# Moving the start of the big buffer to a multiple of 256 bytes, and of the accumulator to a multiple of 64, in a decode kernel that streams its key and value cache

## The chip, the cores and the metric

The kernel runs on one core of a Trainium2 chip. The metric is the device time of one execution in microseconds (us), lower being better. Times are medians of several executions; the profile is one further execution, recorded by the hardware profiler.

## What is computed

One token is decoded. Its normalised vector goes through attention over a long cache and, beside that, through a small mixer and MLP; the results are summed.

```python
def _A_ref(x, k_cache, v_cache, wq, wo):          # Hq 32, Hkv 4, Sk 65536, Dh 128, D 1024
    q = (x @ wq).reshape(B, Sq, Hq, Dh).transpose(0, 2, 1, 3)
    k = jnp.repeat(k_cache, rep, axis=1)           # 8 query heads share one key/value head
    v = jnp.repeat(v_cache, rep, axis=1)
    scores = jnp.einsum("bhqd,bhkd->bhqk", q, k) * (Dh ** -0.5)
    o = jnp.einsum("bhqk,bhkd->bhqd", _softmax(scores), v)
    return o.transpose(0, 2, 1, 3).reshape(B, Sq, Hq * Dh) @ wo

def _B_ref(x, w1, w2, w3, w4):                     # F 3584
    h = _gelu(_layernorm(x) @ w1)
    hs = shifted_quarters_of(h) @ w2               # one position only, so the shifts give zeros
    x1 = x + hs
    return x1 + _gelu(_layernorm(x1) @ w3) @ w4

x = A_x
xn = _layernorm(x)
return x + _A_ref(xn, A_k_cache, A_v_cache, A_wq, A_wo) + _B_ref(xn, B_w1, B_w2, B_w3, B_w4)
```

Nearly all of the bytes are the cache: 4 heads x 65,536 positions x 128 values x 2 bytes, once for K and once for V, are 134 MB of the 170 MB that are read. The rest is weights.

## The kernel before, in words

The kernel is written engine by engine. Small queue objects (`_Q`) collect each engine's instructions with the semaphore waits that follow from buffer objects (`_B`), and the order of work is written out by hand. There is no scheduler that could reorder it.

**Memory.** SBUF tensors are allocated one after the other with `sb(...)` (lines 217 to 261), each starting on a multiple of 32 bytes of the partition. The last is `KV` (line 261), 196,608 bytes of each of the 128 partitions. Everything large is loaded into it. It holds two K buffers and two V buffers of 32,768 bytes (`KOFF`, `VOFF`, line 262), a region for transposed K (`XOFF`), and a region for weights (`WOFF`). All of these offsets, and the places of the weights, are multiples of 256 bytes from KV's start.

**Loads.** SP issues all large transfers, `issue_k` and `issue_v` through line 335 and the weights through line 323. A K or V transfer is 4,096 KB: 16,384 positions of a head, 128 of them in each partition, one contiguous 32,768-byte run per partition. First come wq, K 0, V 0 and K 1; then, as buffers come free, K and V in turn; near the end w1, w2, w3, wo and w4, the last in four parts (line 646) into KV.

**The loop.** One sub-block is 8,192 positions, half of a transfer, and there are 32 of them (`for n in range(NT)`, line 584):

- `Ttr` (line 490): four VectorE transposes of K inside KV, 128x1024 words each, one sub-block ahead.
- `QK` (line 500): 16 TensorE matmuls from the transposed K in KV into `S_ps`.
- `stats1`, `MB`, `stats2` (lines 509 to 519) and `EXP` (lines 528 to 534): the running bound of the softmax on VectorE, the exponential on ScalarE into `p_sb`, with the row sums going to `tmpO`.
- `PTr` (lines 538 and 540): a TensorE permutation and a VectorE transpose of the probabilities into `pT_f`.
- `PV` (line 548): 16 matmuls of V in KV into `OT_ps`.
- `FLASH` (lines 556 to 561): ScalarE copies `OT_ps` to `tmpO`; POOL scales the accumulator `O_acc` by `ff` (line 559) and adds `tmpO` (line 561). At the end of a head, POOL folds `O_acc` into `keep` (`head_end`, lines 566 to 576).

SP's issue of the next K or V transfer stands at the end of a sub-block and waits for the reader of the buffer that it overwrites: the transposes of line 490 for K, the matmuls of line 548 for V.

**The end.** Attention's result goes through `keep` and `o_bf` into the rows of wo (line 660), followed by the rows of w4 (lines 660 and 452) as its parts land; sums go to `OUT_ps` (line 691), and line 696 copies the result for the last DMA.

**Start bytes in a partition, from the built program:** `KV` 31,552, which is 123 x 256 + 64. `O_acc` 26,400, which is 412 x 64 + 32. `tmpO` 20,096, `p_sb` 22,176, `pT_f` 24,224, `keep` 28,480.

Of the kernel before, what the change touches and what calls it, by code (L numbers as in the profile page):

```python
# [6 lines left out]
BF = mybir.dt.bfloat16  # L7
F32 = mybir.dt.float32
# [156 lines left out]
def _dma(q, chan, fn, reads=(), writes=(), partial=False):  # L165
    _deps(q, reads, writes)
    chan.n += 1
    ev = q.dma(fn, chan.sem, 16 * chan.n)
    _done(ev, reads, writes, partial)
    return ev  # L170


def bass_parallel_sum__gqa_block_cached__mixer_s_mlp__decode_kernel(
# [13 lines left out]
    P = 128  # L187
# [17 lines left out]
    with ExitStack() as es:  # L205
        E = es.enter_context

        def sb(name, shape, dt):
            return E(nc.sbuf_tensor(name, shape, dt))
# [30 lines left out]
        qT_bf = sb("qT_bf", [P, HQ], BF)  # L240
        Yall = sb("Yall", [P, HKV, 4, 4, G], BF)
        Ycur = sb("Ycur", [P, 4, 4, G], BF)
        tmpO = sb("tmpO", [P, 520], F32)
        p_sb = sb("p_sb", [P, 2, 512], BF)
        pT_f = sb("pT_f", [P, 512], F32)
        mrow = sb("mrow", [P, 2], F32)
# [11 lines left out]
        acc = sb("acc", [P, KT_D], F32)  # L258
        g_bf = sb("g_bf", [P, KT_D], BF)
        gh_bf = sb("gh_bf", [P, KT_F], BF)  # L260
        KV = sb("KV", [P, 98304], BF)
        KOFF, VOFF, XOFF, WOFF = (0, 32768), (16384, 49152), 65536, 81920
        EPI = KV[:, 45056:49152].bitcast(F32)
        Dmat_f, Pmat_f = EPI[:, 1024:1152], EPI[:, 1152:1280]
# [29 lines left out]
        def chan(name):  # L294
            if name not in chans:
                chans[name] = _DmaChan(sem("d_" + name))
            return chans[name]
# [27 lines left out]
        _dma(q_act, chan("x"), lambda e: e.dma_start(out=x_bf[:, :], in_=A_x[0, 0, :].rearrange("(p j) -> p j", p=P)), writes=[b_x])  # L325
        wq_sb = KV[:, VOFF[1]:VOFF[1] + 8 * HQD]
        b_wq = [b_V[1]] + b_X[0] + b_X[1]
        load_rows(wq_sb, b_wq, "wq", A_wq, 0, 8)

        def issue_kv(m, cache, off, bufs, ch):  # L330
# [3 lines left out]
            src = cache[0, h, nb * 2 * SUB:(nb + 1) * 2 * SUB, :].rearrange("(p c) d -> p (c d)", p=P)  # L334
            _dma(q_sp, chan("%s%d" % (ch, m % 2)), lambda e: e.dma_start(out=KV[:, off:off + 16384], in_=src), writes=bufs)

# [142 lines left out]

        KV32 = KV[:].bitcast(F32)  # L480
        kstep = KV[:].ap[0][0]
        pT_bf = pT_f[:].bitcast(BF).rearrange("p (q r two) -> p q r two", q=16, two=2)
# [10 lines left out]
        def QK(n):  # L493
            xs = n % 2
            fns = []
            for we in range(4):
                w_hi, e_ = divmod(we, 2)
                for cm in range(4):
                    mv = bass.AP(KV[:].tensor, XOFF + xs * 8192 + cm * 128 + w_hi * 64 + e_, [[kstep, P], [512, 16], [2, 32]])
                    fns.append(lambda e, we=we, cm=cm, mv=mv: e.matmul(  # L500
# [232 lines left out]
```

## Time and profile before

| | |
|---|---|
| median of 3 runs | 402.64 us (402.51 to 402.99) |
| the profiled execution | 403.04 us, of which the span from first to last instruction is 401.7 us |
| read from device memory | 169.87 MB, 423 GB/s over the span |
| VectorE (DVE) busy | 238.7 us (59%), 403 instructions |
| TensorE (PE) busy | 183.4 us (46%), 1428 matmuls |
| GpSimd (POOL) busy | 92.2 us (23%), 175 instructions |
| ScalarE (ACT) busy | 49.7 us (12%), 132 instructions |
| mean granted TensorE clock | 0.635 of full speed |

The page of a profile lists, for one execution, busy times by engine, the span in 40 equal slices, the DMA queues, the chain of work that ended last, the costliest groups of instructions (line, engine, operation, output<-input, count, busy us, mean ns, idle time before and what ended it), and the large transfers with the time from issue to landing. The trace behind it can be asked for one line, one stretch of time or one queue, and it holds a record of every DMA packet with its bytes and duration. A busy share is a mean over stages with different limits, so the chain and the waits are read with it.

### The profile page before, as it was taken

To read this page: it belongs to the slowest core of one execution; us is meant where nothing else is said; L and a number is where in the kernel's file an instruction comes from. 1 tells how busy PE (TensorE), PEld (TensorE's weight loads), DVE (VectorE), ACT (ScalarE), POOL (GpSimd) and SP (SyncE) were. 2 spreads that over 40 slices of the span, in tenths; PEclk is the share of its full clock that TensorE was granted. 3 is DMA by queue.
4 is the path that set the end of the run, shared out by engine and by line. 5 is a ranking of instruction groups with operands and counts; after the bars stand their busy time and mean duration, and the time that the engine had idled before them with its cause. 6 is when DMAs were issued, how large, how long until landed. Compare 5 with 4: busy or idle time off the path is not lost.

```text
span 401.7 us, 4260 instructions
## 1 busy us (share of the span) xinstructions
PE 183.4 (46%) x1428; PEld 52.9 (13%) x1428; DVE 238.7 (59%) x403; ACT 49.7 (12%) x132; POOL 92.2 (23%) x175
## 2 busy tenths in 40 slices
PE   0043256463534444444444454545352636636557
PEld 0022011110111111111111011111010101212112
DVE  0024788667575758585768585858585858664201
ACT  1000011111111111111112020111111112100000
POOL 6000032231315222222432121216222222430000
PEclk9998556555655555656566555566566565585988
DMA  9989999999999999999999999999999999999995
GB/s 385 450 365 434 447 417 424 450 427 424 427 447 421 428 434 440 421 427 444 431 427 431 440 424 431 434 437 422 427 447 431 424 424 427 465 398 427 439 413 212
DMA packets 6209, 169.98 MB, mean 423 GB/s; under 512 B 820, under 2 KB 824, under 8 KB 952
## 3 DMA queue, kind: packets, MB, share of 16 engines
q1 hardware_dynamic: 6056, 169.87, 98.5%
q8 instruction: 4, 0.07, 0.1%
q14 instruction: 5, 0.04, 0.0%
q10 hardware_dynamic: 144, 0.00, 0.0%
HBM read 169.87 MB, written 0.00 MB: 423 GB/s over the span
## 4 chain that ended last, share of the span: by engine, by line
DMA 56%; DVE 19%; PE 11%; issue 11%; ACT 1%; POOL 0%; DVEq 0%; SPq 0%; ACTq 0%; POOLq 0%
DMA KV<-in_A_k_cache_dram 41%; DVE KV L490 12%; DMA KV<-in_B_w_dram 10%; DMA x_bf<-in_A_x_dram 6%; PE S_ps L500 5%; DVE mrow L509 3%; PE PT_ps L538 2%; PE S_ps L660 2%; ACT p_sb L530 1%; PE MB_ps L515 1%; DVE Bst L519 1%; DVE Rm L510 1%; DVE brun L528 1%; DVE pT_f L540 1%; PE OT_ps L548 0%
## 5 line engine op out<-in xcount | busy, mean ns | idle before, releaser
L490 DVE STREAM_TRANSPOSE KV<-KV 128x1024 f32<-128x1024 f32 x132 | 156.5, 1216 | 53.9 <-DMA KV<-in_A_k_cache_dram 53.9
L548 PE MATMUL OT_ps<-KV,pT_f 128*32 128x512 bf16 x512 | 60.7, 627 | 26.6 <-DVE pT_f L540 26.6
L500 PE MATMUL S_ps<-KV,Ycur 128*32 128x512 bf16 x512 | 59.2, 610 | 16.9 <-DVE KV L490 16.9
L561 POOL TENSOR_TENSOR O_acc<-O_acc,tmpO 128x516 f32<-128x516 f32 x32 | 41.3, 1290 | 95.8 <-ACT tmpO L556 95.8
L530 ACT ACTIVATE p_sb<-S_ps,brun 128x512 bf16<-128x512 f32 x32 | 22.0, 688 | 163.9 <-DVE brun L528 163.9
L515 PE MATMUL MB_ps<-Rm,Lmat 128*128 128x16 bf16 x32 | 6.2, 192 | 75.6 <-DVE Rm L510 75.6
L538 PE MATMUL PT_ps<-p_sb,permR 128*128 128x512 bf16 x32 | 18.3, 571 | 45.8 <-ACT p_sb L530 45.8
L556 ACT ACTIVATE tmpO<-OT_ps 128x512 f32<-128x512 f32 x32 | 19.1, 598 | 106.1 <-PE OT_ps L548 106.1
L558 POOL TENSOR_TENSOR spare<-ff 128x1 f32<-128x1 f32 x32 | 6.2, 193 | 113.1 <-ACT ff L534 113.0
L509 DVE TENSOR_REDUCE mrow<-S_ps 128x1 f32<-128x512 f32 x32 | 21.6, 675 | 16.5 <-PE S_ps L500 16.5
L540 DVE STREAM_TRANSPOSE pT_f<-PT_ps 128x512 f32<-128x512 f32 x32 | 22.7, 709 | 3.0
L500 PEld LDWEIGHTS S_ps<-KV,Ycur 128*32 128x32 bf16 x512 | 14.7, 125 | 62.1 <-issue 32.4
L548 PEld LDWEIGHTS OT_ps<-KV,pT_f 128*32 128x32 bf16 x512 | 14.8, 129 | 58.6 <-DVE pT_f L540 30.7
L559 POOL TENSOR_SCALAR O_acc<-O_acc,ff 128x520 f32<-128x520 f32 x32 | 22.3, 698 | 0.0
L515 PEld LDWEIGHTS MB_ps<-Rm,Lmat 128*128 128x128 bf16 x32 | 3.3, 102 | 103.0 <-DVE Rm L510 103.0
L381 PE MATMUL MM_ps<-ln_s,ones_f 128*128 128x1 f32 x6 | 1.8, 362 | 27.2 <-DVE ln_s L380 27.2
L689 DVE COPY KV<-S_ps 64x512 f32<-64x512 f32 x1 | 0.7, 683 | 22.1 <-PE S_ps L660 22.1
L377 DVE CAST xT<-x_bf 128x8 f32<-128x8 bf16 x1 | 0.2, 173 | 21.5 <-DMA x_bf<-in_A_x_dram 21.5
L660 PE MATMUL S_ps<-KV,o_bf 128*1 128x512 bf16 x64 | 8.9, 443 | 5.0 <-DMA KV<-in_A_wo_dram 5.0
L519 DVE TENSOR_REDUCE Bst<-MB_ps 128x1 f32<-128x16 f32 x32 | 5.6, 175 | 9.2 <-PE MB_ps L515 9.2
L393 POOL TENSOR_TENSOR ln_s<-ln_s,neghalf 128x1 f32<-128x1 f32 x3 | 1.7, 558 | 39.5 <-DVE ln_s L391 39.5
L538 PEld LDWEIGHTS PT_ps<-p_sb,permR 128*128 128x128 bf16 x32 | 3.3, 103 | 48.7 <-ACT p_sb L530 48.7
(116 smaller groups left out, 127.0 us busy)
## 6 DMA issues: line engine op xcount, KB each, us to landing
KV<-in_A_k_cache_dram SPq DMA_DIRECT2D x16, 4096.0 KB, 23.3
KV<-in_A_v_cache_dram SPq DMA_DIRECT2D x16, 4096.0 KB, 22.1
KV<-in_A_wo_dram SPq DMA_DIRECT2D x2, 4096.0 KB, 27.4
KV<-in_B_w_dram SPq DMA_DIRECT2D x1, 7168.0 KB, 20.9
KV<-in_B_w_dram SPq DMA_DIRECT2D x2, 2048.0 KB, 24.9
KV<-in_B_w_dram SPq DMA_DIRECT2D x1, 4096.0 KB, 41.3
KV<-in_B_w_dram SPq DMA_DIRECT2D x1, 1536.0 KB, 41.3
KV<-in_B_w_dram SPq DMA_DIRECT2D x1, 1024.0 KB, 43.4
```

The lines of the kernel that those rows point to most:

```text
L490: _op(q_dve, lambda e, c=c, x=x: e.transpose(out=KV32[:, x:x + 1024], in_=KV32[:, c:c + 1024]), reads=[b_K[s][half]], writes=[b_X[xs][ix]])
L500: fns.append(lambda e, we=we, cm=cm, mv=mv: e.matmul(S_ps[32 * cm:32 * cm + 32, :], Ycur[:, we, :, :].rearrange("p a g -> p (a g)"), mv, s ...
L509: _op(q_dve, lambda e: e.reduce_max(mrow[:, m:m + 1], S_ps[:, :], axis=AX.X), reads=[b_S], writes=[b_mrow[m]])
L515: _op(q_pe, lambda e: e.matmul(MB_ps[:, 0:16], Lmat[:, :], Rm[:, m, :], start=True, stop=True), reads=[b_R[m], b_const], writes=[b_MB])
L530: _op(q_act, lambda e: e.activation(p_sb[:, m, :], S_ps[:, :], ACTF.Exp, bias=brun[:, m:m + 1], scale=SCALE, accum_out=tmpO[:, cL:cL + 1]) ...
L538: _op(q_pe, lambda e: e.matmul(PT_ps[:, :], permR[:, :], p_sb[:, m, :], start=True, stop=True), reads=[b_p[m], b_const], writes=[b_PT])
L540: _op(q_dve, lambda e: e.transpose(out=pT_f[:, :], in_=PT_ps[:, :]), reads=[b_PT], writes=[b_pT])
L548: fns.append(lambda e, q=q, q4=q4: e.matmul(OT_ps[32 * q4:32 * q4 + 32, :], pT_bf[:, q, :, 1], KV[:, v0 + 512 * q:v0 + 512 * (q + 1)], sta ...
L556: _op(q_act, lambda e: e.activation(tmpO[:, 4:516], OT_ps[:, :], ACTF.Copy), reads=[b_OT], writes=[b_tmpO])
L559: b_Oacc.set_write(q_pool.op(lambda e: e.tensor_scalar(out=O_acc[:, :], in0=O_acc[:, :], scalar1=ff[:, m:m + 1], scalar2=0.0, op0=ALU.mult ...
L561: ev = q_pool.op(lambda e: e.tensor_tensor(out=O_acc[:, 4 * m:4 * m + 516], in0=O_acc[:, 4 * m:4 * m + 516], in1=tmpO[:, 4 * m:4 * m + 516 ...
L660: _grp(q_pe, [lambda e, lhs=lhs, rhs=rhs, jj=jj: e.matmul(S_ps[32 * jj:32 * jj + 1, :], lhs, rhs[:, 512 * jj:512 * jj + 512], start=False, ...
```

## The change

`tmpO` is allocated with 528 elements in place of 520, 32 bytes more, and a tensor `align` of 160 bytes, which nothing uses, is allocated ahead of `KV`. Everything allocated after `tmpO` moves up by 32 bytes, and `KV` by 192.

```diff
-        tmpO = sb("tmpO", [P, 520], F32)
+        tmpO = sb("tmpO", [P, 528], F32)
...
         gh_bf = sb("gh_bf", [P, KT_F], BF)
+        sb("align", [P, 80], BF)
         KV = sb("KV", [P, 98304], BF)
```

| tensor | start before | start after |
|---|---|---|
| `tmpO` | 20,096 (multiple of 64) | the same |
| `p_sb` | 22,176 (multiple of 64, plus 32) | 22,208 (multiple of 64) |
| `pT_f` | 24,224 (multiple of 64, plus 32) | 24,256 (multiple of 64) |
| `Rm` | 26,304 (multiple of 64) | 26,336 (multiple of 64, plus 32) |
| `O_acc` | 26,400 (multiple of 64, plus 32) | 26,432 (multiple of 64) |
| `keep` | 28,480 (multiple of 64) | 28,512 (multiple of 64, plus 32) |
| `brun` | 31,104 (multiple of 64) | 31,136 (multiple of 64, plus 32) |
| `o_bf` | 31,360 (multiple of 64) | 31,392 (multiple of 64, plus 32) |
| `KV` | 31,552 (multiple of 256, plus 64) | 31,744 (multiple of 256) |

No instruction is added, removed or reordered on any engine, and no other code changes.

## Prediction, made before the changed kernel had run

> **What bounds the kernel now.** I read the page from the top: engine shares first, then the slices and the queues. The busiest engine, VectorE (DVE), is busy 59% of the span; the transfers are another matter. These are the DMA lines of the page (busy tenths and GB/s in 40 slices of 10.04 us, then the main queue with its packets, MB and share of 16 DMA engines):
>
> ```profile
> DMA  9989999999999999999999999999999999999995
> GB/s 385 450 365 434 447 417 424 450 427 424 427 447 421 428 434 440 421 427 444 431 427 431 440 424 431 434 437 422 427 447 431 424 424 427 465 398 427 439 413 212
> q1 hardware_dynamic: 6056, 169.87, 98.5%
> ```
>
> The reader is to see that the 16 DMA engines never pause between the first slices and the last. 98.5% of 401.7 us is 395.7 us of packets on every engine. Next question: does a compute engine hold the transfers back? The DMA queue's own waits (who waited for whom; us in total, times, longest) and the issues (KB each, median us from issue to landing):
>
> ```profile
> SPq L335 <- PE OT_ps L548: 144.8, 14, 11.0
> SPq L335 <- DVE KV L490: 126.6, 14, 21.6
> ...
> KV<-in_A_k_cache_dram SPq DMA_DIRECT2D x16, 4096.0 KB, 23.3
> KV<-in_A_v_cache_dram SPq DMA_DIRECT2D x16, 4096.0 KB, 22.1
> ```
>
> SP does wait, for VectorE and TensorE to free a buffer. But it issues each transfer 22 to 23 us before it lands. The chain of waits gives the pace (start us, length us, what):
>
> ```profile
> 107.69 23.52 DMA KV<-in_A_k_cache_dram
> ...
> 146.78 23.30 DMA KV<-in_A_k_cache_dram
> ...
> 185.64 23.30 DMA KV<-in_A_k_cache_dram
> ...
> 224.08 23.72 DMA KV<-in_A_k_cache_dram
> ```
>
> From 107.69 to 224.08 are three rounds of 38.80 us, each of two K and two V transfers of 4.19 MB: 9.70 us per transfer. A transfer is therefore issued 23.3 - 9.7 = 13.6 us before its turn comes. A compute engine must be late by about 13.6 us before a DMA engine runs dry; it gains nothing by being early. The time is the sum of the packets, then a tail, of which this is the same chain's end:
>
> ```profile
> 391.15 6.38 PE S_ps L660 x42
> ...
> 398.60 0.61 PE OUT_ps L691 x8
> 399.20 0.35 PE OUT_ps L452 x8
> ...
> 399.57 0.42 DVE p_sb L696
> ```
>
> The tail begins at the landing of part 0 of w4, so all of it moves with the transfers.
>
> **What a packet costs.** The change touches where packets are written, so I split their time with the trace's packet records (bytes and duration of each). Medians: 159 ns for 4,096 bytes, 309 for 8,192, 613 for 16,384, 1,215 for 32,768, 2,418 for 65,536. From the shortest to the longest: (2418 - 159) / (65536 - 4096) = 0.03677 ns per byte, and 159 - 4096 x 0.03677 = 8.4 ns that do not depend on the length. By the shapes, each engine gets 336 data packets: 8 for each of 32 K and V transfers, 8 each for wq and w3, 16 for wo, 8 each for w1 and w2, and 32 for the four parts of w4. Check of the sum: 169.87 MB / 16 x 0.03677 ns = 390.4 us; 336 x 8.4 ns = 2.8 us; 43 small completion packets of 9 ns = 0.4 us; packets over their size's median, nearly all at starts of transfers, 2.1 us: 395.7 us, as the page says.
>
> **The change, part by part.** No instruction is added, removed or moved on any queue; every engine's list of instructions is the same in both programs apart from line numbers. Only start bytes move.
>
> *KV from byte 31,552 (64 past a multiple of 256) to 31,744 (a multiple of 256).* Every large transfer writes into KV at a multiple of 256 bytes from its start, so all 336 packets of an engine are aligned after and none before. The trace has no aligned large packet, so I bound. The 390.4 us that grow with length can't show a cost per line crossed: packets of 4 KB and of 64 KB pay the same per byte, and nothing in the records isolates alignment there. What a start can cost once per packet is at most the constant: 336 x 8.4 = 2.8 us gain. Against that end stand packets that do not touch KV: the 4-byte completion packets and the 16-byte packets of x_bf take 9 ns as well. So about all of the constant is there without KV, and the gain is near 0. What may be left: 32,768-byte packets, 280 of the 336, take 1215 - 32768 x 0.03677 = 10.1 ns over their bytes, 1.1 ns above the 9. 1.1 x 280 = 0.3 us. I take a gain of 0.3 us, the value nearest to the small packets' row. The loss end: the 32,768-byte group has its 95th percentile at 1,222 ns; if all packets went there, 7 x 336 = 2.4 us slower.
>
> [...]
>
> *What reads KV.* In the stream, transposes (1,216 ns each, 16 per round), matmuls of L500 and L548: VectorE is busy 26.1 to 26.9 us of a 38 to 40 us stretch by the stage table, and the cover is the 13.6 us. Gain 0, cost 0. In the tail the 42 matmuls of 6.38 us read KV on the path; the 44 of that line on w4 rows run 377 to 631 ns, median 379, so 0.5% either way, 0.03 us; at nothing.
>
> *O_acc from 32 past a multiple of 64 to a multiple of 64.* Its readers and writers are on POOL (count | busy us, mean ns | idle before, releaser):
>
> ```profile
> L561 POOL TENSOR_TENSOR O_acc<-O_acc,tmpO 128x516 f32<-128x516 f32 x32 | 41.3, 1290 | 95.8 <-ACT tmpO L556 95.8
> L559 POOL TENSOR_SCALAR O_acc<-O_acc,ff 128x520 f32<-128x520 f32 x32 | 22.3, 698 | 0.0
> ```
>
> Were L561 as quick as L559, POOL would save 32 x 0.59 = 18.9 us and wait as much longer for ScalarE; were it doubled, POOL would have 92.2 + 41.3 = 133.5 us in 401.7. POOL idles 3 to 6 us before the next sub-block's first instruction. On the path: 0 either way.
>
> *What rides along.* The 32 bytes also move p_sb and pT_f to multiples of 64, and keep, brun, Rm and o_bf off them. Their instructions are 0.2 to 0.7 us each inside a round with 13.6 us of cover; keep and o_bf in the tail are used before wo lands, where TensorE waits 5.0 us for that transfer. At nothing; without the cover a change of 5% of the 0.7 us transposes of pT_f would be 32 x 0.035 = 1.1 us.
>
> **Sum.** The profiled execution took 403.04 us (span 401.7 and 1.3 around it), 0.4 above the median 402.64. 403.04 - 0.3 = 402.7; against the median 402.3.
>
> **Rivals.** (1) *The constant falls.* Each packet loses 2.4 ns or more: 336 x 2.4 = 0.8 us, which is 0.2%, about what a measurement of this kernel can tell from no change. At half the constant, 4.2 x 336 = 1.4 us: 401.2; at the whole, 399.8. For: nothing else bounds the stream, so every ns of every packet counts 336 times. Against: the 9 ns of packets that have nothing to do with KV. (2) *Slower, at the packets' write side.* With every packet of all 16 engines starting on the same boundary, writes meet each other or the engines' reads more often. The price is 336 times the lengthening: from 2.4 ns it shows (403.5), at the 1,222 ns of the group's slow end 405.0. For: 32 KB packets spread from 1,213 to 1,222 ns, so something already lengthens some. Against: that spread is 0.7%, and the stage table has 431 GB/s in a stretch with POOL busy 12.2 us and 430 in the next one with 8.0. (3) *VectorE becomes the bound* by slower transposes. It would need (38.8 - 26.4) / 16 = 0.78 us more on each of 1.22 us; doubled, 26.4 + 16 x 1.22 - 38.8 = 7.1 us in each of 8 rounds, near 459 us. Nothing speaks for it: KV starts on a multiple of 64 before and after. (4) *The change does nothing at all:* the start bytes in the program say that it moves both buffers, so this is only the low end of my forecast.
>
> **Numbers.** Forecast, within 0.8 us of 402.6 with a small gain likeliest: 0.56. Rival 1: 0.29. Rival 2: 0.13. Rival 3: 0.02. So faster 0.29, same 0.56, slower 0.15. The likeliest case alone spans 401.8 to 403.4. The range goes to 400.8 (5.5 ns per packet gained) and 403.8 (3.5 ns lost), leaving out the far ends of rivals 1 and 2 and rival 3, near 0.15 in all.
>
> **What would show it.** Right: 32 KB packets at 1,213 to 1,215 ns, rounds of 38.7 to 38.8 us, the main queue still near 98.5%, POOL rows changed or not without a trace in the end. Rival 1: 1,207 to 1,212 ns. Rival 2: 1,218 ns or more, rounds of 38.9 or more. Rival 3: DMA slices below 9 in mid-span. A different price per byte, which I have no row to exclude at another start, would make me wrong by 3.9 us for each 1%.

## The result, and the profile after

The changed kernel took 402.19 us (median of 14 runs, 401.0 to 402.61) against 403.16 us for the kernel before (14 runs beside it, 402.51 to 404.05). The ratio is 0.9969, with a 95% interval of 0.9957 to 0.9980: a gain of 1.25 us, between 0.8 and 1.7 (the two medians alone differ by 0.97). The time lies inside the range, and even inside the span given for the likeliest case, 401.8 to 403.4. The gain, though, is not the 0.3 us of that case: the 32,768-byte packets, most of the stream, lost over 2.4 ns on the mean, as shown below, and that is rival 1, given 0.29.

The page of the changed kernel, DMA lines (busy tenths and GB/s in 40 slices; the main queue with packets, MB and share of 16 engines):

```profile
span 400.6 us, 4244 instructions
...
DMA  9989999999999999999999999999999999999995
GB/s 386 439 380 429 452 418 425 448 431 422 432 452 419 433 432 442 425 429 448 425 432 432 445 425 429 432 442 423 429 455 422 432 435 421 454 411 429 430 414 217
...
q1 hardware_dynamic: 6056, 169.87, 98.6%
```

The same bytes in the same packets, the engines as full as before, in a span 1.1 us shorter. So the packets themselves got shorter. The slices can't show it: neighbouring slices swing by 10% (454 and 411 GB/s), and the change is 0.3%. The chain of waits (start us, length us, what) shows a little:

```profile
107.69 23.07 DMA KV<-in_A_k_cache_dram
...
146.32 23.13 DMA KV<-in_A_k_cache_dram
...
184.78 23.40 DMA KV<-in_A_k_cache_dram
...
223.74 23.16 DMA KV<-in_A_k_cache_dram
```

Three rounds now take 116.05 us, 38.68 each, where they took 38.80. The tail follows the transfers (same chain, its end):

```profile
389.98 6.62 PE S_ps L661 x44
...
397.43 0.61 PE OUT_ps L692 x8
398.04 0.35 PE OUT_ps L453 x8
...
398.41 0.42 DVE p_sb L697
```

It starts 1.17 us earlier and its last piece 1.16 us earlier: nothing was gained or lost in it. POOL's two rows of the loop on the accumulator (count | busy us, mean ns | idle before, releaser) stand still:

```profile
L562 POOL TENSOR_TENSOR O_acc<-O_acc,tmpO 128x516 f32<-128x516 f32 x32 | 41.3, 1290 | 96.5 <-ACT tmpO L557 96.5
...
L560 POOL TENSOR_SCALAR O_acc<-O_acc,ff 128x520 f32<-128x520 f32 x32 | 22.5, 702 | 0.0
```

1,290 ns as before, and 702 against 698. The accumulator's new start makes neither quicker.

What changed stands in the packet records of the two traces. 32,768-byte packets, 4,480 of each kernel, duration in ns:

```
                      5%    25%   median  75%   95%    mean   mean, 52 to 325 us
before                1213  1214  1215    1218  1222   1217.1  1216.8
after                 1213  1213  1213    1213  1213   1213.9  1213.0
```

(The last column leaves out packets over 1,260 ns, 6 in each kernel.) Before, nine packets in ten took something between 1,213 and 1,222 ns. After, 4,428 of 4,480 take exactly 1,213. 3.2 ns x 280 packets are 0.9 us; with the 16,384-byte packets (616.0 to 611.9, 16 per engine, 0.07 us) and the rest, the packets of an engine, of all queues, add up to 395.5 us in place of 396.5. One us of the 1.25 is seen directly.

### The profile page after: what moved, and what is told of

It is laid out like the page before. It is cut to its first block, busy times and chain, and to the rows that moved or that the text cites. A ratio compares the mean times of both kernels' runs of the same rounds, so it can differ in the third digit from the quotient of the medians.

```text
span 400.6 us, 4244 instructions
## 1 busy us (share of the span) xinstructions
PE 175.3 (44%) x1412; PEld 53.0 (13%) x1428; DVE 239.1 (60%) x403; ACT 49.7 (12%) x132; POOL 92.8 (23%) x175
## 4 chain that ended last, share of the span: by engine, by line
DMA 56%; DVE 21%; issue 11%; PE 10%; ACT 1%; DVEq 0%; POOL 0%; SPq 0%; another core or an unknown queue 0%; ACTq 0%; POOLq 0%
DMA KV<-in_A_k_cache_dram 40%; DVE KV L491 14%; DMA KV<-in_B_w_dram 10%; DMA x_bf<-in_A_x_dram 6%; PE S_ps L501 5%; DVE mrow L510 3%; PE S_ps L661 2%; PE PT_ps L539 1%; ACT p_sb L531 1%; PE MB_ps L516 1%; DVE Rm L511 1%; DVE Bst L520 1%; DVE brun L529 1%; DVE pT_f L541 1%; PE OT_ps L549 0%
## 5 line engine op out<-in xcount | busy, mean ns | idle before, releaser
L562 POOL TENSOR_TENSOR O_acc<-O_acc,tmpO 128x516 f32<-128x516 f32 x32 | 41.3, 1290 | 96.5 <-ACT tmpO L557 96.5
L539 PE MATMUL PT_ps<-p_sb,permR 128*128 128x512 bf16 x16 | 9.7, 608 | 22.8 <-ACT p_sb L531 22.8
```

The source lines that it names most:

```text
L539: _op(q_pe, lambda e: e.matmul(PT_ps[:, :], permR[:, :], p_sb[:, m, :], start=True, stop=True), reads=[b_p[m], b_const], writes=[b_PT])
L562: ev = q_pool.op(lambda e: e.tensor_tensor(out=O_acc[:, 4 * m:4 * m + 516], in0=O_acc[:, 4 * m:4 * m + 516], in1=tmpO[:, 4 * m:4 * m + 516 ...
```

## The experiments

Each kernel was timed against the kernel before on the same chip. "Mean packet" is always that of 32,768-byte packets landing mid-stream, 52 to 325 us, packets over 1,260 ns left out: 1,216.8 before, 1,213.0 after.

### One half of the change at a time

Theory A was that the start of the packets' writes decides, theory B that the accumulator and the small tensors do. KV alone:

```diff
+        sb("align", [P, 96], BF)
         KV = sb("KV", [P, 98304], BF)
```

> Only KV moves, to 31,744, a multiple of 256; the accumulator and all tensors ahead of KV stay where they were. Theory A (the start of the packets' writes decides): ratio to the kernel before 0.997, 32,768-byte packets in mid-stream all near 1,213 ns as in the changed kernel. Theory B (the accumulator, the probabilities and their neighbours decide, because the engines' accesses to them get in the way of something): ratio 1.000, packets spread from 1,213 to 1,222 ns with a mean near 1,216.8 as before.

Measured: ratio 0.9967 (0.9955 to 0.9979), mean packet 1,213.0 ns. The accumulator alone:

```diff
-        tmpO = sb("tmpO", [P, 520], F32)
+        tmpO = sb("tmpO", [P, 528], F32)
...
+        sb("align", [P, 112], BF)
         KV = sb("KV", [P, 98304], BF)
```

> Only the tensors after tmpO move by 32 bytes, the accumulator to a multiple of 64; KV starts at 31,808, which is 64 past a multiple of 256 as before. Theory A: ratio 1.000, mean packet near 1,216.8 ns. Theory B: ratio 0.997, packets near 1,213 ns.

Measured: ratio 0.9998 (0.9985 to 1.001), mean packet 1,216.8 ns. Theory A stands, B falls. The whole gain is KV's start. POOL's L562 row in the KV-only kernel, with the accumulator at its old place:

```profile
L562 POOL TENSOR_TENSOR O_acc<-O_acc,tmpO 128x516 f32<-128x516 f32 x32 | 41.2, 1289 | 96.7 <-ACT tmpO L557 96.7
```

### Which multiple it takes

KV 128 past a multiple of 256, by a tensor of 64 bytes ahead of it (`sb("align", [P, 32], BF)`):

> Only KV moves, to 31,616, which is 128 past a multiple of 256. Theory A1 (any start off a multiple of 256 splits a write at the boundary and costs alike): ratio 1.000, mean packet near 1,216.8 ns. Theory A2 (a multiple of 128 is enough): ratio 0.997, 1,213 ns.

Measured: ratio 0.9989 (0.9977 to 1.0001), mean packet 1,217.0 ns. The ratio alone would not decide between A1 and A2, but the packets do: they are as long as before. KV 96 past a multiple of 256 (`[P, 16]`):

> Only KV moves, to 31,584, which is 96 past a multiple of 256 and 32 past a multiple of 64. Theory A1: ratio 1.000, mean packet near 1,216.8 ns. Rival A3 (the cost grows with a finer misalignment, a multiple of 64 being better than one of 32): ratio 1.003 or more, mean packet 1,220 ns or more.

Measured: ratio 0.9996 (0.9985 to 1.0008), mean packet 1,216.9 ns. KV at an odd multiple of 256 (`[P, 224]`):

> The full computation; only KV moves, to 32,000, an odd multiple of 256 (the changed kernel's 31,744 is a multiple of 1,024 as well). Theory A (a multiple of 256 is enough): ratio 0.997 to the kernel before, packets at 1,213 ns. Rival A5 (a multiple of 512 or 1,024 is needed): ratio 1.000, mean near 1,216.8 ns.

Measured: ratio 0.9965 (0.9953 to 0.9978), mean packet 1,213.1 ns. A multiple of 256 is enough; 64, 96 and 128 bytes past it cost the same 3.8 to 4.0 ns per packet. Finally 16 bytes past, off every multiple of 32:

```diff
-        KV = sb("KV", [P, 98304], BF)
+        sb("align", [P, 96], BF)
+        KVa = sb("KV", [P, 98312], BF)
+        KV = KVa[:, 8:98312]
...
-                    mv = bass.AP(KV[:].tensor, XOFF + xs * 8192 + ...
+                    mv = bass.AP(KV[:].tensor, 8 + XOFF + xs * 8192 + ...
```

> The full computation; everything in KV begins 16 bytes past a multiple of 256 (31,760), so not even on a multiple of 32. Theory A1 (a start off a multiple of 256 costs the same wherever it lies): ratio 1.000 to the kernel before, mean packet near 1,216.8 ns. Rival A4 (a start off a multiple of 32 costs more, since each piece of a write is cut as well): mean packet 1,230 ns or more, ratio 1.01 or more.

Measured: ratio 1.0019 (1.0006 to 1.0032), mean packet 1,219.4 ns. Neither expectation holds. It costs about 2.5 ns more per packet than the other starts off a multiple of 256, and far less than the 1,230 ns that rival A4 expected. Why 16 bytes past costs more than 64, no run here shows. Nor does any show a write split at the boundary, as theory A1 has it, or cut further, as rival A4 has it: both were the author's guesses, and the runs give durations alone.

### Do the engines have a part in it?

In the trace of before, the packets are exactly 1,213 ns long up to 45 us, and only then begin to lengthen, just when transposes (40.9 us) and score matmuls (45.7 us) are starting. So theory C was that the engines' work on SBUF lengthens misaligned packets, that is, packets written from a start off a multiple of 256 bytes. The loop's arithmetic was taken out, leaving the loads:

```diff
-            QK(n)
-            Ttr(n + 1, [0])
...
-            PV(n)
-            FLASH(n)
```

> KV starts at 31,552 as before (64 past a multiple of 256). The whole loop's arithmetic is left out (transposes, scores, softmax, values, accumulation; a reciprocal at the end is a copy); all loads stay, and each waits only for the landing of the transfer it overwrites. In the kernel before, packets of the first transfers took 1,213 ns and those from 46 us on a mean of 1,216.8. Theory C (misaligned packets are lengthened by the engines' work on SBUF): mean 1,213.0 ns from start to end. Rival D (they lengthen by themselves once the DMA engines have drifted apart or transfers queue behind one another): mean near 1,216.8 ns in mid-stream without any engine at work.

Measured: ratio 0.9996 (0.9983 to 1.001), mean packet 1,216.8 ns. The page of this kernel, busy tenths of TensorE, VectorE, ScalarE, POOL and the DMA engines:

```profile
PE   0161000000000000000000000000000001445667
...
DVE  0206200000000000000000000000000000642001
ACT  1000000000000000000000000000000000000000
POOL 6002910000000000000000000000000000000000
...
DMA  9989999999999999999999999999999999999995
```

The reader is to see two things. No compute engine works between the sixth slice and the thirty-fourth, and the misaligned packets are as long as ever: theory C falls. And the time without any of the loop's arithmetic is that of the full kernel, so all of that work is hidden. Two more kernels put back one engine each, transposes alone (`Ttr(n + 1, [0, 1, 2, 3])`) and matmuls alone (`QK(n)`, `PV(n)`):

> As the run with loads only, but the four VectorE transposes of each sub-block stay, and the K loads wait for them as before. Theory C with VectorE as the cause: mean near 1,216.8 ns in mid-stream. Theory C with TensorE as the cause: 1,213.0. Rival D: near 1,216.8, as with loads only.

Measured: ratio 0.9988 (0.9975 to 1.0002), mean packet 1,216.8 ns.

> As the run with loads only, but the 16 score matmuls and the 16 value matmuls of each sub-block stay (on data that is not rewritten), and the V loads wait for them. Theory C with TensorE as the cause: mean near 1,216.8 ns in mid-stream. Theory C with VectorE as the cause: 1,213.0. Rival D: near 1,216.8.

Measured: ratio 0.9996 (0.9981 to 1.0011), mean packet 1,216.7 ns. All three have early packets of 1,213 ns too, lengthening from 45 us on. Of rival D, the part that needs no engine holds. The drift does not: in the trace of before, the first six of the 16 engines' packets start 0, 29, 128, 147, 153 and 223 ns after the first of them at 24 us, and just the same at 48 us, when packets had already begun to lengthen. Nor do transfers that queue behind one another: SP issues four of them at the start (before; start us, length us, what), and the 32,768-byte packets up to 45 us all take 1,213 ns.

```profile
0.79 0.39 SPq L323 DMA_DIRECT2D KV<-in_A_wq_dram  x1
1.24 0.41 SPq L335 DMA_DIRECT2D KV<-in_A_k_cache_dram  x1
1.70 0.43 SPq L335 DMA_DIRECT2D KV<-in_A_v_cache_dram  x1
2.17 0.68 SPq L335 DMA_DIRECT2D KV<-in_A_k_cache_dram  x1
```

### Why only from 45 us on?

Theory E: each misaligned packet puts the write side of an engine a few ns further behind its read side, and the records show it only when the slack between the two is used up. Then a pause should give the slack back. The run with loads only, with one pause:

```diff
+            if ch == "k" and m == 10:
+                for c in ("k0", "k1", "v0", "v1"):
+                    q_sp.wait((chan(c).sem, 16 * chan(c).n))
```

> The run with loads only (KV at 31,552, arithmetic of the loop left out), with one pause: SP issues K transfer 10 only when everything before it has landed. Theory E (the write side of a DMA engine loses 3.8 ns on every misaligned packet; slack between read and write hides that until it is used up, at the start after the 28 packets or so that an engine has had by 46 us; a pause gives the slack back): after the pause packets of 1,213 ns for 25 to 30 packets of each engine, 30 to 37 us, then a mean near 1,216.8 again. Rival F (packets are longer from the second use of a buffer on, or from some time on, whatever went before): a mean near 1,216.8 right after the pause.

Measured: 406.39 us (two runs), 3 us more than without the pause; mean packet (ns) by transfer, with the start of each in us (the first packet of each engine after the pause, 1,408 to 2,079 ns, is over 1,260 ns and so left out):

```
start   196.7   206.4  | 219.4   229.7   239.4   249.1   258.7   268.4   278.1
mean   1216.8  1217.0  | 1213.4  1213.2  1213.0  1213.0  1214.5  1216.6  1217.0
```

SP's queue shows where the pause lay (start us, length us, what):

```profile
218.45 0.33 SPq L338 DMA_DIRECT2D KV<-in_A_k_cache_dram  x1
218.82 0.43 SPq L338 DMA_DIRECT2D KV<-in_A_v_cache_dram  x1
```

Between the end of the last packet before it and the start of the first one after it lie 1.5 us. The packets after it are back at 1,213 ns, and lengthen again from 261 to 263 us on, after 42 to 44 us or some 35 packets of each engine: 25 to 30 had been expected. Rival F falls. The course is the one that theory E forecast, the run of short packets somewhat longer. A fixed time of some 43 us since the packets last began would fit the start and the pause as well, but not the other runs: the 16-byte start lengthens from 36 us on, and the halved packets below from 34. A fixed sum of what the packets cost fits all of them roughly: the 16-byte start costs 6.4 ns per packet and lengthens some 20 packets into an engine's work (128 ns in all), the 64-byte start at 3.8 ns after 28 (106 ns), and after the pause after 35 (133 ns). Eight of the first 20 and 28 are packets of wq, of 65,536 bytes, counted like the others. That what is used up is a buffer between the read and the write side is argued from this, not shown.

### Per packet or per byte?

Each K and V transfer, and that of w1, was issued as two of half the size, which makes two packets of 16,384 bytes out of one:

```diff
-            _dma(q_sp, chan("%s%d" % (ch, m % 2)), lambda e: e.dma_start(out=KV[:, off:off + 16384], in_=src), writes=bufs)
...
+            q_sp.dma(lambda e: e.dma_start(out=KV[:, off:off + 8192], in_=src[:, 0:8192]), c.sem, 16 * (c.n - 1))
+            _done(q_sp.dma(lambda e: e.dma_start(out=KV[:, off + 8192:off + 16384], in_=src[:, 8192:16384]), c.sem, 16 * c.n), [], bufs)
```

> The full computation, KV at 31,552 as before; each K and V transfer, and w1, is issued as two of half the size, so 32,768-byte packets become pairs of 16,384 bytes: 264 packets more per engine, and 33 completion packets of 9 ns. Theory per packet (each packet costs 8.4 ns, and 3.7 more when misaligned): 264 x 12.1 ns + 0.3 us = 3.5 us more than the kernel before, ratio 1.0087; 16,384-byte packets at a mean of 614.5 ns. Rival per byte (misalignment costs by length): 16,384-byte packets at 612.9, and 264 x 8.4 ns + 0.3 us = 2.5 us more, ratio 1.0062.

> As the run with halved transfers, but KV at 31,744, a multiple of 256. Theory per packet: 611.0 ns per 16,384-byte packet; against the run with halved transfers at 31,552 it gains 600 packets x 3.7 ns = 2.2 us, twice what the change gains; ratio to the kernel before 1.003. Rival per byte: it gains the same 1.2 us as the change; ratio 1.003.

Measured: halved and misaligned, ratio 1.0062 (1.0048 to 1.0076), 405.26 us, packets of 614.8 ns mid-stream. Halved and aligned, ratio 1.0005 (0.9995 to 1.0016), 403.22 us, 611.0 ns. With twice the packets aligning gains 2.0 us by the medians and 2.3 by the ratios, where the change gains 1.25: the cost is one of packets, not of bytes. The gain between the two runs and the packets' means (614.5 and 611.0 forecast per packet, 612.9 for the first per byte) decide this. The ratios to the kernel before do not: 1.0062 is what the rival forecast, and 1.0005 is below the 1.003 of both. In the misaligned run the packets begin to lengthen at 34 us instead of 45, again after some 28 packets of an engine. The main queue of the two, misaligned first:

```profile
q1 hardware_dynamic: 10808, 169.88, 98.9%
```

```profile
q1 hardware_dynamic: 10808, 169.88, 98.5%
```

They missed because the 8.4 ns that both took for a packet's own cost were too high. From the KV-only kernel at 0.9967 to the halved aligned one at 1.0005 are 1.5 us for 264 packets and 33 completions, 5.8 ns for each packet (3.4 to 8.2 by the intervals of the two ratios). By the records two packets of 611.0 are 9 ns longer than one of 1,213. The traces don't settle it: against the changed kernel's, the stream from the first K packet's start to the last data packet's end grew by 1.3 us and the sum of its packets by 2.0; against the KV-only kernel's, by 2.0 and 2.3; and the halved aligned execution that was profiled, 404.69 us, was the longest of its 12. How much of a packet's 8 ns is really serial stays open.

## Why the prediction was right or wrong, step by step

**What bounds the kernel: right.** The loads alone take the time of the whole kernel. The tail moved with the transfers, by 1.17 us.

**The engines and the accumulator at nothing: right.** POOL's rows did not change, and moving the accumulator alone gives 0.9998.

**The packet's constant: the place was right, the size wrong, and with it the likeliest case.** The step that failed is "1.1 x 280 = 0.3 us", where the packets lost 3.2 ns each on the mean and the kernel 1.25 us. It failed twice. I took the median of a skewed group, 1,215, where a sum over packets needs the mean, 1,217.1. And I took the 9 ns of the 4-byte and 16-byte packets as the floor of an aligned large packet. The floor stood in the same trace: the 1,213 ns at the quick end of the group, and of every packet before 45 us. 1217.1 - 1213 = 4.1 ns over 280 packets is 1.15 us, near the 1.25 that were measured; 0.2 us of it are ten packets of over 1,260 ns, of which the changed kernel has some too. That aligning would bring all packets to this floor the trace could not tell, since the packets before 45 us were misaligned as well. The bound of the whole constant, 2.8 us, held.

**The check of the sum hid it.** It booked 2.1 us as packets over their size's median, "nearly all at starts of transfers". The records of before give 1.9 us, and 0.5 us of that are 32,768-byte packets only 1 to 30 ns over their median, all of them after 45 us: the cost in question.

**The time itself was met by luck.** The forecast against the median was 402.3 us, and 402.19 were measured. But the three runs behind the 402.64 were quicker than the 14 beside the result (403.16), by 0.5 us, which made up for about half of the gain that was missed.

**Rival 2 read its own evidence backwards.** It took the spread from 1,213 to 1,222 ns as a sign that "something already lengthens some". It did: the misaligned start. The spread was the cost that the change removes, and it vanished: 4,428 of 4,480 packets at 1,213 ns. It was evidence for rival 1. That writes or reads meet more often when all packets start alike was its guess; no run shows it.

**What would show it: badly chosen.** For rival 1 I asked for packets of 1,207 to 1,212 ns. The quickest packets stayed at 1,213; the slow ones disappeared. Both 1,213 ns and rounds of 38.68 us stood in the list as signs of the likeliest case.

**Writes alone were tested.** The runs show a cost on the write side of 3.8 to 4.0 ns per packet, alike at 64, 96 and 128 bytes past a multiple of 256 (1,216.8, 1,216.9 and 1,217.0 ns against 1,213.0). No run moved the start of what is read.

## What to carry to other kernels

Where a profile shows the DMA engines full from end to end, look at the distribution of the packets' durations, not at their median: packets of equal size that spread by a few ns may pay a cost that the quickest of them do not, and the difference of mean and minimum times their number is then about what can be won. Here that was 1.15 us, and 1.25 were gained. Start a buffer that long transfers land in on a multiple of 256 bytes of the partition: it cost 192 bytes of each partition here and gave 0.3% at 336 packets per engine, 0.5% at 600 (405.26 to 403.22 us, by the medians). Aligning what the other engines work on gave nothing here (0.9998), where the engines have 13.6 us of cover.

## What was not expected of the hardware

In these runs a misaligned packet is not charged at once. At 64 bytes past a multiple of 256 the first 28 or so packets of an engine are as short as aligned ones (1,213 ns for 32,768 bytes), at 16 bytes past the first 20 or so; after a pause of 1.5 us between packets some 35 are short again; then each costs 3.8 ns more on the mean, in values from 1,213 to 1,222. The first transfers alone show no cost: in the traces before and after alike, wq's packets have a median of 2,418 ns, and those of K 0 and V 0 take 1,213. And a start 16 bytes past a multiple of 256 (1,219.4 ns) costs more than one 64, 96 or 128 bytes past it (1,216.8 to 1,217.0).
